# Quest chunk-select attention into a capacity-limited MoE: bounds a round later, first loads on two queues, key casts on ScalarE, expert rows turned one ahead

## Chip, core and metric

One Trainium2 chip, one core. The metric is device time in microseconds (us) of one execution of the kernel. "TensorE clock" below is the clock that the throttle granted, as a share of full speed, as the profile records it.

## The reference

Attention first, for B = 4, H = 8, S = 768, D = 64. Keys are cut into 24 chunks of 32. For each query, each chunk has an upper bound of its score, and only the six chunks with the highest bound (among those that the causal mask allows) are attended to. Then a mixture of experts, top-1 of 8, where each expert keeps the 80 tokens of highest gate weight and all other rows of the output are zero.

```python
ub = sum(maximum(q[..., None, :] * k_min, q[..., None, :] * k_max), -1)   # chunk bounds
ub = where(causal, ub, -1e9); top = argsort(ub)[..., -6:]
scores = q @ k.T / sqrt(64), kept where chunk in top and query >= key
x = softmax(scores) @ v                     # reshaped to 3072 x 512
logits = x @ w_gate; expert = argmax(logits); gate = softmax(logits)[expert]
for e in range(8):
    idx = the 80 tokens of expert e with the highest gate
    out[idx] = gate[idx] * (relu(x[idx] @ w1[e]) @ w2[e])   # F = 1024
```

## The kernel before

**Units of work.** The 32 heads are worked in 8 quads of four heads (g = 0 to 7), two quads to a batch entry. The 768 queries of a head are three thirds of 256 (t = 0, 1, 2), and each pair of a third and a pair of 128-key blocks is a round: one round for t = 0, two for t = 1, three for t = 2. So a quad has six rounds (r = 0 to 5) and the kernel 48 (rd = 6g + r). The third is complete at r = 0, 2 and 5.

**A round.** TensorE computes the scores of four heads (L352 to L373: keys by queries at L366, then at L370 a penalty of -30000 for chunks that were not selected, from `ind` and `PENT`) into four PSUM buffers, one for each head, of a pool `psS` that has just four. ScalarE takes the exponentials (L381, one for each head, into `E`); on the rounds of the diagonal, r = 0, 2 and 4, GpSimd masks them (L385). TensorE multiplies by the values of the round before (L390 to L403, into `ps_num`) and sums the denominators (L405 to L417, into `ps_den`). When a third is complete, ScalarE copies `ps_num` out (`npt`, L421); two rounds later the gate's logits are added from `npt` (`gate_rows`, L424, `DSB`), three rounds later VectorE gets denominators and logits (`scales`, L435 to L457, with the reductions `den` at L444), four rounds later TensorE turns the rows (`ps_xn`, L465), VectorE scales them (`x_nat`, L466) and they go to DRAM (L472). In odd quads, `scales` ends in `best` (L477: the row's maximum and the exponential `ex`, L489, on ScalarE) and, at the start of a later round, `gates` (L508) which writes `gmask`, `gs` and `slotrhs`.

**Preparing the next quad** (`prep`, L240) goes on beside this, with the keys and queries that the DMA has laid out as `kn` and `qn`:

- K step f (f = 0, 1): VectorE turns half of the keys (L250, 32x32 transposes, `kT`), GpSimd casts them to bf16 in another element order (`KB`, L266; its input has a stride of 32 elements), VectorE takes minimum and maximum over each chunk (L270). f = 0 is issued in r = 0, f = 1 in r = 1.
- Q step f: VectorE turns queries (L250, `qT`), ScalarE takes their positive part (`qp`, L276), GpSimd casts (`QB`, L278). Both in r = 2.
- `bound` (L294): 1152 small matmul instructions over the 8 quads (L310), into the same four `psS` buffers as the scores, and four transposes by VectorE (`ub`, L314). In r = 3, between `value` and `denom`.
- `rank` (L316): VectorE takes the eight highest bounds of each query and compares (`PEN`, L320). In r = 4.
- `unselect` (L324): TensorE turns `PEN` (`ps_pen`, L327), ScalarE copies it (`PENT`, L329). In r = 5, ahead of `value`.

`KB`, `QB`, `PEN` and `PENT` have two copies each, one for even and one for odd quads. `kT`, `qT`, `qp` have one.

**Loads.** All loads of keys, queries and values (L218 to L238) and the zero fill of the output (`zero_fill`, L130, 12 DMAs of 512 KB at r = 3, 4, 5 of quads 1 to 4) are issued by SyncE; weights of 1 MB a piece by GpSimd (L145, `load_whole` at r = 2 and 4, `late_weights` from rd 40 on, into tiles that are spent by then, the zero tile among them). The first keys and the first queries are loaded in three parts of four DMAs (L873, L874), and quad 0's keys are turned by thirds.

**Selecting while attention runs.** After quads 3 and 5, three generators sort the gate weights: `lanes1` (L571) sorts 96 lanes 128 wide, `lanes2` (L581) 64 lanes 160 wide, `lanes3` (L592) 40 lanes 288 wide. Each step is one VectorE maximum of eight and one replacement (L550, L552), and ten steps give 80 values. A generator is appended four rounds after the round that completed its third, and four steps are issued at each round's end (L951). From rd 42 (`FREEZE`) on, `freeze` (L611) has the threshold `ps_tau` and the places of the first three batch entries.

**The tail.** After the last round: `turn_new` (L706), `weigh1`, `rows`, `turn_new(2)`, `weigh2` (L785: TensorE spreads gates over rows, VectorE and GpSimd compare and count, `ps_idx` at L824 gives the indices of the rows kept). Then GpSimd gathers each expert's 80 rows (`X`, L976); `hidden` (L980) turns them on TensorE (`ps_XT`, L984), copies them on ScalarE (`XT`, L987) and multiplies by w1 (`ps_H`, L994); `result` (L1004) multiplies by w2 (`ps_Y`, L1008), scales (`Y`, L1011) and scatters (L1013). The order on TensorE is hidden(0), hidden(1), result(0), hidden(2), result(1) and so on.

**Who sets the order.** The order of TensorE and of SyncE's queue is the program's order throughout, VectorE's too until the last round (L870 to L872, L955). ScalarE's and GpSimd's instructions are put in order by the scheduler, each as its engine and its inputs are estimated to be ready. In the changed kernel as built, the scheduler puts both key casts of quad 1 ahead of round 0's exponentials; from quad 1 on it puts r = 0's cast ahead of that round's exponentials, right behind `PENT`, and r = 1's cast behind `npt`, ahead of r = 1's exponentials. In even quads both `qp` stand ahead of r = 3's exponentials; in odd quads the first stands ahead of r = 2's, and the second, with `npt`, behind r = 3's.

## Time and profile before

| what | value |
|---|---|
| two timed runs | 344.68 and 346.19 us, median 345.44 |
| the profiled execution | 341.36 us; span of the trace 339.6 us |
| mean granted clock of TensorE | 0.936 |
| half clock (0.5) | 67.18 to 70.59, 101.31 to 104.72, 224.19 to 227.60, 237.84 to 244.67, 275.39 to 278.80, 285.63 to 306.11 us |
| first score of rd 0 | 21.72 us |
| start of quads 1 to 7 (row turn at r = 0) | 50.1, 80.0, 112.25, 144.3, 174.2, 204.15, 245.0 us |
| first rows gathered, first `ps_H` | 296.69, 300.36 us |
| idle time of TensorE in gaps over 0.2 us | 53.3 us |
| longest of these gaps within the quads | 4.60 us at 234.48, 3.18 at 270.93, 2.77 at 98.80, 2.31 at 133.90, 1.99 at 264.33, 1.94 at 220.44 |
| in the tail | 3.02 us at 284.83, 3.33 at 291.71, 3.34 at 296.00, then 0.52 to 0.59 for each expert |
| `gmask` (VectorE, L522) | 0.18 us, but 3.70 at 92.06 and 4.06 at 155.84, while GpSimd ran the cast of `QB` |
| DMA | 47.82 MB, 141 GB/s over the span |

How to read the profile: PE is TensorE's matmuls, PEld its weight loads, DVE is VectorE, ACT ScalarE, POOL GpSimd, SP SyncE, and a trailing q means an engine's sequencer or queue. L366 is line 366 of the kernel. A row of the page's slices has 40 digits, the busy share of each fortieth of the span in tenths; PEclk is the granted clock in the same way. A row of waits reads: the waiting engine and its operation, who ended the wait, the total in us, how many, and the longest. A row of a timeline: start, length, engine, line, operation, out<-in, shape, how many, and in brackets the idle time of the engine before it with what ended it ("issue" is no wait that the trace shows).

### The profile page before, as it was taken

What the parts mean: (1) busy time and instruction counts of PE and PEld (TensorE: products, weight loads), DVE (VectorE), ACT (ScalarE), POOL (GpSimd) and SP (SyncE); (2) the same over time, 40 slices, a digit from 0 to 9 for tenths busy, and PEclk for the clock granted to TensorE, in tenths of its full rate; (3) what the DMA queues carried; (4) which work ended last, traced back from release to release, by engine and by line L of the source; (5) the groups of instructions that cost most, each with busy time, mean ns of one, the idle gap of its engine ahead of it and who ended that gap; (6) DMA issues with size and microseconds to landing.
All of it is one profiled execution on the core that took longest, in us unless ns stands there. A gap on an engine that the chain in (4) does not pass through costs nothing. (4 is left out here: it accounts for less than half of the span.)

```text
span 339.6 us, 12569 instructions
## 1 busy us (share of the span) xinstructions
PE 270.0 (80%) x5316; PEld 169.8 (50%) x5316; DVE 198.2 (58%) x697; ACT 141.8 (42%) x325; POOL 150.1 (44%) x315
## 2 busy tenths in 40 slices
PE   0349999799969986999999899766899675468881
PEld 0226666466636654565555566443456343255550
DVE  3666248358754754389796478976964845412230
ACT  1126356626723752566257347344164225412220
POOL 6936227635732562368118344664062101072222
PEclk9999999989998999999999999979599978559998
DMA  3799207995998299759949955699963001021121
GB/s 109 167 220 210 48 2 152 224 266 168 225 235 266 63 228 282 180 145 218 271 157 226 220 111 128 100 154 181 189 97 66 33 1 64 1 58 41 41 58 30
DMA packets 59367, 47.82 MB, mean 141 GB/s; under 512 B 27974, under 2 KB 51654, under 8 KB 59312
## 3 DMA queue, kind: packets, MB, share of 16 engines
q1 hardware_dynamic: 45776, 28.36, 33.3%
q0 software_dynamic: 13536, 18.67, 31.4%
q8 instruction: 41, 0.67, 0.9%
q14 instruction: 14, 0.11, 0.1%
HBM read 53.10 MB, written 10.76 MB: 188 GB/s over the span
## 5 line engine op out<-in xcount | busy, mean ns | idle before, releaser
L381 ACT ACTIVATE E<-ps_S 128x384 f32<-128x384 f32 (+1 forms) x192 | 91.5, 550 | 70.0 <-PE ps_S L370 70.0
L398 PE MATMUL ps_num<-E,vn 128*32 128x256 f32 (+1 forms) x1536 | 93.6, 365 | 0.8 <-issue 0.8
L398 PEld LDWEIGHTS ps_num<-E,vn 128*32 128x32 f32 x1536 | 51.2, 112 | 31.4 <-issue 5.6
L385 POOL TENSOR_SCALAR_AFFINE_SELECT E<-E 128x256 f32<-128x256 f32 x96 | 38.7, 434 | 52.0 <-ACT E L381 51.8
L414 PE MATMUL ps_den<-E,ones 128*32 128x256 f32 (+1 forms) x768 | 56.0, 371 | 4.0 <-issue 2.8
L414 PEld LDWEIGHTS ps_den<-E,ones 128*32 128x32 f32 x768 | 29.1, 116 | 19.9 <-issue 7.2
L266 POOL CAST KB<-kT 128x768 bf16<-128x768 f32 x16 | 25.1, 1570 | 30.3 <-DVE kT L250 21.0
L366 PE MATMUL ps_S<-QB,KB 32*128 32x256 bf16 (+1 forms) x768 | 35.3, 264 | 0.8 <-ACT E L381 0.8
L466 DVE TENSOR_TENSOR x_nat<-ps_xn,rec 128x512 bf16<-128x512 f32 x24 | 16.5, 687 | 27.3 <-PE ps_xn L465 22.4
L370 PE MATMUL ps_S<-PENT,ind 32*128 32x256 bf16 (+1 forms) x384 | 25.1, 257 | 2.7 <-issue 2.3
L278 POOL CAST QB<-qT 128x768 bf16<-128x768 f32 x16 | 24.4, 1545 | 3.6 <-DVE qT L250 3.5
L314 DVE STREAM_TRANSPOSE ub<-ps_u 128x160 f32<-128x160 f32 x32 | 8.3, 318 | 26.9 <-PE ps_u L310 26.9
L366 PEld LDWEIGHTS <-KB 32*128 32x128 bf16 x768 | 16.4, 94 | 14.9 <-issue 14.0
L276 ACT ACTIVATE qp<-qT 128x640 f32<-128x640 f32 x16 | 11.7, 749 | 19.8 <-DVE qT L250 19.5
L250 DVE STREAM_TRANSPOSE kT<-kn 128x768 f32<-128x768 f32 (+1 forms) x17 | 15.7, 923 | 6.8 <-DMA kn<-in_k_dram 6.7
L310 PE MATMUL ps_u<-ind,later 32*32 32x160 bf16 x128 | 6.4, 245 | 16.0 <-DVE later L79 8.0
L310 PE MATMUL ps_u<-qT,KMM 32*32 32x160 f32 x512 | 14.3, 444 | 6.0 <-DVE qT L250 6.0
L421 ACT ACTIVATE npt<-ps_num 128x512 f32<-128x512 f32 x24 | 14.8, 615 | 10.0 <-PE ps_num L398 10.0
L465 PE MATMUL ps_xn<-ident_f,npt 128*128 128x128 f32 x96 | 16.7, 300 | 0.9 <-DVE lg_h L451 0.7
L310 PE MATMUL ps_u<-qp,KMM 32*32 32x160 f32 x512 | 17.3, 446 | 0.0
L1013 POOL DMA_INDIRECT out_dram<-Y,sidx x8 | 7.4, 919 | 22.0 <-DVE Y L1011 13.3
L489 ACT ACTIVATE ex<-sh 128x16 f32<-128x16 f32 x12 | 2.6, 215 | 34.6 <-DVE sh L486 34.6
(217 smaller groups left out, 420.2 us busy)
## 6 DMA issues: line engine op xcount, KB each, us to landing
w<-in_moe_w_dram POOLq DMA_DIRECT2D x11, 1024.0 KB, 13.4
vn<-in_v_dram SPq DMA_DIRECT2D x32, 192.0 KB, 3.4
out_dram<-zero_tile SPq DMA_DIRECT2D x12, 512.0 KB, 12.0
kn<-in_k_dram SPq DMA_DIRECT2D x28, 192.0 KB, 6.9
qn<-in_q_dram SPq DMA_DIRECT2D x28, 192.0 KB, 9.0
x_dram<-x_nat SPq DMA_DIRECT2D x12, 257.0 KB, 3.0
kn<-in_k_dram SPq DMA_DIRECT2D x12, 64.0 KB, 1.9
qn<-in_q_dram SPq DMA_DIRECT2D x12, 64.0 KB, 1.9
```

Source lines behind the costliest of these rows:

```text
L250: nc.vector.transpose(out=dst[:, fs, 32 * xs.start:32 * xs.stop].rearrange("p f (x t) -> p x f t", t=CHUNK), in_=src[:].rearrange("p c (i ...
L266: nc.gpsimd.tensor_copy(out=straight(KB[s][:, f, :]), in_=natural(kT[:, f, :]))
L278: nc.gpsimd.tensor_copy(out=straight(QB[s][:, f, :]), in_=natural(qT[:, f, :]))
L310: nc.tensor.matmul(out=ps_u[h][32 * j:32 * (j + 1), :, :], lhsT=lhsT, rhs=rhs[rs, j], start=(w == 0), stop=(w == 2 and f == 1), skip_group ...
L366: nc.tensor.matmul(out=ps_S[h][:, m, 0:wid], lhsT=KB[s][rs, w, keys], rhs=QB[s][rs, w, q0:q0 + wid], start=(w == 0), stop=False, skip_grou ...
L370: nc.tensor.matmul(out=ps_S[h][:, m, lo - q0:wid], lhsT=ind[rs, keys], rhs=PENT[s][rs, lo - P:q0 + wid - P], start=False, stop=True, skip_ ...
L381: nc.scalar.activation(out=E[:].rearrange("p m q -> p (m q)")[:, 0:last], in_=ps_S[h][:].rearrange("p m q -> p (m q)")[:, 0:last], func=my ...
L385: nc.gpsimd.affine_select(out=E[:, :, 0:P], in_=E[:, :, 0:P], compare_op=ALU.is_ge, fill=0.0, base=0, pattern=[[0, 2], [1, P]], channel_mu ...
L398: nc.tensor.matmul(out=NUM[q0:q0 + 32, a, c0:THIRD], lhsT=nats[(g, "vn")][:, kb, 2 * a + r, 32 * f:32 * (f + 1)], rhs=Es[rd][2 * a + r][:, ...
L414: nc.tensor.matmul(out=dn[q0:q0 + 32, c0:THIRD], lhsT=ones32[:, a, :], rhs=Es[rd][2 * a + r][:, m, 0:wid], start=(i == 0 and x == 0), stop ...
L465: nc.tensor.transpose(ps_xn[:, j, a, :], npt[:, a, j * P:(j + 1) * P], ident_f32[:])
L466: nc.vector.tensor_tensor(out=xbuf[(b, t)][:, :, P * gi:P * (gi + 1)].bitcast(BF16).rearrange("p j (k d) -> p j k d", d=HEAD_D), in0=ps_xn ...
```

## The change

- The first loads are six DMAs of 128 KB for the keys on SyncE's queue and six for the queries on ScalarE's.
- The cast of `KB` is an activation (Copy) on ScalarE instead of a GpSimd copy.
- Q step 0 is issued in r = 2 and Q step 1 in r = 3; `bound` in r = 4, `rank` in r = 5, `unselect` at the end of r = 5, behind `denom`.
- `gates` is called at the end of the round before the one at whose start it stood. Generators are appended a round earlier, and their steps (3 or 4 a round) are issued between the `after` list and `value`.
- `lanes1` also sorts its own merge of 160 values (32 lanes), and `lanes2` sorts 128 wide (32 lanes) and merges.
- The two reductions of `den` become one.
- The zero fill is issued at the even rounds 16 to 38.
- 31 matmuls of 512 columns that compute nothing that is used (`idle`, into the spent `ps_num`): ten ahead of `turn_new(2)`, ten ahead of `ps_idx`, eleven behind it.
- The turn of an expert's rows is issued one expert ahead, behind `hidden(e)` and ahead of `result(e - 1)`.

```diff
@@ -217,16 +217,17 @@
 
-        def load(g, src, name, parts=1):
+        def load(g, src, name, engine=None):
             dst = qkp.tile([P, QBLK, 4 * HEAD_D], F32, name=name)
-            n = QBLK // parts
-            for i in range(parts):
+            if engine:
+                for c in range(QBLK):
+                    engine.dma_start(out=dst[:, c, :], in_=src[4 * g:4 * g + 4, :, c, :])
+            else:
                 for h in range(4):
-                    nc.sync.dma_start(out=dst[32 * h:32 * (h + 1), n * i:n * (i + 1), :],
-                                      in_=src[4 * g + h, :, n * i:n * (i + 1), :])
+                    nc.sync.dma_start(out=dst[32 * h:32 * (h + 1), :, :], in_=src[4 * g + h])
             nats[(g, name)] = dst
 
-        def load_k(g, parts=1):
-            load(g, k4, "kn", parts)
+        def load_k(g, engine=None):
+            load(g, k4, "kn", engine)
 
-        def load_q(g, parts=1):
-            load(g, q4, "qn", parts)
+        def load_q(g, engine=None):
+            load(g, q4, "qn", engine)
 
@@ -265,3 +266,4 @@
             def keys(f):
-                nc.gpsimd.tensor_copy(out=straight(KB[s][:, f, :]), in_=natural(kT[:, f, :]))
+                nc.scalar.activation(out=straight(KB[s][:, f, :]), in_=natural(kT[:, f, :]),
+                                     func=mybir.ActivationFunctionType.Copy)
                 kv = kT[:, f, :].rearrange("p (c i j t) -> p c j i t", i=4, j=4, t=8)
@@ -442,5 +444,4 @@
             dv = ps_dT[:].rearrange("p j (w r c) -> p j c r w", w=2, r=2)
-            for a in range(2):
-                nc.vector.tensor_reduce(out=den[:, :, a, :], in_=dv[:, :, a],
-                                        axis=mybir.AxisListType.X, op=ALU.add)
+            nc.vector.tensor_reduce(out=den[:], in_=dv[:, :, 0:2], axis=mybir.AxisListType.X,
+                                    op=ALU.add)
             rec = small.tile([P, 2, 4], F32, name="rec")
@@ -565,3 +566,3 @@
         L1 = cand[0][0:96, P:P + CAP]
-        S2, L2 = lane(0, 64, 208, 160), lane(0, 64, 368, CAP)
+        S2, L2 = lane(0, 32, 208, 160), lane(0, 32, 368, CAP)
         S3, L3 = lane(0, 40, 448, 288), lane(0, 40, 736, CAP)
@@ -575,6 +576,6 @@
             nc.vector.tensor_copy(out=back, in_=rev(cand[0][32:64, P:P + CAP]))
-            nc.vector.tensor_tensor(out=S2[0:32, 0:CAP], in0=L1[0:32, :], in1=back, op=ALU.max)
-            nc.vector.tensor_copy(out=S2[0:32, CAP:160], in_=L1[64:96, :])
-            nc.gpsimd.memset(cand[0][32:64, 208 + P:208 + 160], -1.0)
+            nc.vector.tensor_tensor(out=S2[:, 0:CAP], in0=L1[0:32, :], in1=back, op=ALU.max)
+            nc.vector.tensor_copy(out=S2[:, CAP:160], in_=L1[64:96, :])
             nc.gpsimd.memset(S3, -1.0)
+            yield from sort_lanes(S2, L2)
 
@@ -582,5 +583,5 @@
             copied(cand[0][32:64, 208:208 + P], turned(12, 4)[:])
-            yield from sort_lanes(S2, L2)
+            yield from sort_lanes(cand[0][32:64, 208:208 + P], cand[0][32:64, 368:368 + CAP])
             nc.vector.tensor_copy(out=back, in_=rev(cand[0][32:64, 368:368 + CAP]))
-            nc.vector.tensor_tensor(out=M3, in0=L2[0:32, :], in1=back, op=ALU.max)
+            nc.vector.tensor_tensor(out=M3, in0=L2, in1=back, op=ALU.max)
             for i in range(4):
@@ -784,2 +785,7 @@
 
+        def idle(n):
+            for _ in range(n):
+                nc.tensor.matmul(out=NUM[:].rearrange("p a q -> p (a q)"), lhsT=ident_bf[:],
+                                 rhs=ties[:, 0:2 * THIRD], start=True, stop=True)
+
         def weigh2():
@@ -823,2 +829,3 @@
                                     op=ALU.is_equal)
+            idle(10)
             ps_idx = misc([CAP, 2, NEXP], F32, "ps_idx")
@@ -831,2 +838,3 @@
                                  start=False, stop=(c == NEWB - 1), skip_group_check=True)
+            idle(11)
             left = selp.tile([CAP, NEXP], F32, name="left")
@@ -872,4 +880,4 @@
         with tc.manual_schedule(engines=by_hand | {mybir.EngineType.DVE}):
-            load_k(0, 3)
-            load_q(0, 3)
+            load_k(0, nc.sync)
+            load_q(0, nc.scalar)
             nc.sync.dma_start(out=wg_sb[:], in_=moe_w_gate.rearrange("(t r) e -> r t e", r=P))
@@ -890,4 +898,2 @@
                     eg, et = ends[rd - 4]
-                    if eg % 2 == 1:
-                        gates(eg // 2, et)
                     before.append(lambda e=ends[rd - 4]: rows(*e))
@@ -901,8 +907,6 @@
                         after.append(u["K"][1])
-                    elif r == 2:
-                        after += u["Q"]
-                    elif r == 4:
-                        after.append(u["rank"])
+                    elif r in (2, 3):
+                        after.append(u["Q"][r - 2])
                     elif r == 5:
-                        after.append(u["unselect"])
+                        after.append(u["rank"])
                 if r == 1 and 1 <= g < NQUAD - 1:
@@ -913,4 +917,4 @@
                     load_q(g + 2)
-                if r in (3, 4, 5) and 1 <= g <= 4:
-                    zero_fill(3 * (g - 1) + r - 3)
+                if 16 <= rd < 40 and rd % 2 == 0:
+                    zero_fill((rd - 16) // 2)
                 if r in (2, 4) and 1 <= g <= NPRE or r == 2 and g == NPRE + 1:
@@ -927,2 +931,6 @@
                     fn()
+                if merges:
+                    for _ in range((3, 4, 4, 3, 4, 4)[r]):
+                        if merges and next(merges[0], merges) is merges:
+                            merges.pop(0)
                 if rd == FREEZE:
@@ -937,3 +945,3 @@
                     value(rd - 1)
-                if r == 3 and g + 1 < NQUAD:
+                if r == 4 and g + 1 < NQUAD:
                     u["bound"]()
@@ -946,10 +954,11 @@
                         ends[rd - 1] = (gl, t)
-                if rd - 4 in ends:
-                    make = {(3, 2): lanes1, (5, 1): lanes2, (5, 2): lanes3}.get(ends[rd - 4])
+                if r == 5 and g + 1 < NQUAD:
+                    u["unselect"]()
+                if rd - 3 in ends:
+                    eg, et = ends[rd - 3]
+                    if eg % 2 == 1:
+                        gates(eg // 2, et)
+                    make = {(3, 2): lanes1, (5, 1): lanes2, (5, 2): lanes3}.get(ends[rd - 3])
                     if make:
                         merges.append(make())
-                if merges:
-                    for _ in range(4):
-                        if merges and next(merges[0], merges) is merges:
-                            merges.pop(0)
         with tc.manual_schedule(engines=by_hand):
@@ -962,2 +971,3 @@
             rows(*last)
+            idle(10)
             turn_new(2)
@@ -979,4 +989,5 @@
 
-        def hidden(e):
-            w1 = weights[(e, 0)]
+        XTs = {}
+
+        def turn_rows(e):
             ps_XT = psX.tile([P, 4, CAP], BF16, space=bass.MemoryType.PSUM, tag="x", name="ps_XT")
@@ -985,4 +996,8 @@
                                     ident_bf[0:CAP, 0:CAP])
-            XT = mp.tile([P, 4, CAP], BF16, name="XT")
-            nc.scalar.activation(out=XT[:], in_=ps_XT[:], func=mybir.ActivationFunctionType.Copy)
+            XTs[e] = mp.tile([P, 4, CAP], BF16, name="XT")
+            nc.scalar.activation(out=XTs[e][:], in_=ps_XT[:], func=mybir.ActivationFunctionType.Copy)
+
+        def hidden(e):
+            w1 = weights[(e, 0)]
+            XT = XTs.pop(e)
             HT = mp.tile([P, 8, CAP], BF16, name="HT")
@@ -1018,4 +1033,7 @@
         held = None
+        turn_rows(0)
         for e in range(NEXP):
             HT = hidden(e)
+            if e + 1 < NEXP:
+                turn_rows(e + 1)
             if held is not None:
```

## The prediction

> **What bounds the kernel now.** I read the page first, then the waits, the timeline of two quads, and the stretches of the tail.
>
> ```profile
> PE 270.0 (80%) x5316; PEld 169.8 (50%) x5316; DVE 198.2 (58%) x697; ACT 141.8 (42%) x325; POOL 150.1 (44%) x315
> ...
> PEclk9999999989998999999999999979599978559998
> ...
> issue 1%; POOLq 0%; DMA 0%
> ```
>
> TensorE is the fullest engine; the clock falls to half around slices 28 and 34-35. The chain of waits covers 1% of the span, so I followed TensorE's idle time instead. The waits name who ends it:
>
> ```profile
> POOL KB L266 <- DVE kT L250: 21.0, 7, 6.7
> ...
> PE ps_pen L327 <- DVE PEN L320: 8.1, 2, 4.6
> ...
> PE ps_u L310 <- ACT E L381: 7.7, 19, 1.9
> ...
> PE ps_H L994 <- ACT XT L987: 4.6, 8, 0.6
> ```
>
> The third row is what the move of the bounds is after, the fourth what turning rows ahead is after. The first is a wait that the change hands from GpSimd to ScalarE. Now the timeline of rounds 6 and 7:
>
> ```profile
> 49.50 0.66 PE L465 MATMUL ps_xn<-ident_f,npt 128*128 128x128 f32 x4
> ...
> 50.19 0.69 DVE L466 TENSOR_TENSOR x_nat<-ps_xn,rec 128x512 bf16<-128x512 f32 x1 [3.29 <-PE ps_xn L465]
> ...
> 50.80 1.64 ACT L381 ACTIVATE E<-ps_S 128x384 f32<-128x384 f32 x4 [1.15 <-PE ps_S L370]
> 50.80 0.97 DVE L250 STREAM_TRANSPOSE kT<-kn 128x768 f32<-128x768 f32 x1
> ...
> 51.90 1.59 POOL L266 CAST KB<-kT 128x768 bf16<-128x768 f32 x1 [6.42 <-DVE kT L250]
> ...
> 53.37 0.40 PE L366 MATMUL ps_S<-QB,KB 32*128 32x256 bf16 x8
> ...
> 53.53 0.97 DVE L250 STREAM_TRANSPOSE kT<-kn 128x768 f32<-128x768 f32 x1
> ```
>
> Round 6's exponentials run beside the turn of the keys; round 7's scores start at 53.37, 0.93 us after the exponentials' end at 52.44. These scores need the four PSUM buffers that the exponentials free, so 0.93 us is all the slack. Then, out of the timelines of TensorE and VectorE, the fetch gaps, a late key turn and an expert:
>
> ```profile
> 101.57 1.08 PE L414 MATMUL ps_den<-E,ones 128*32 128x128 f32 x11 [2.77 <-issue]
> ...
> 136.21 0.26 PE L370 MATMUL ps_S<-PENT,ind 32*128 32x256 bf16 x1 [2.31 <-issue]
> ...
> 211.29 0.96 DVE L250 STREAM_TRANSPOSE kT<-kn 128x768 f32<-128x768 f32 x1
> ...
> 308.41 1.31 PE L994 MATMUL ps_H<-XT,w 128*128 128x80 bf16 x32 [0.52 <-ACT XT L987]
> ```
>
> Two gaps of TensorE that nothing but its own issue ended, both in rounds with zero fill; a key turn that sorting pushed to 7.1 us after its round's row turn (3.4 in rounds 6 and 7); and 0.52 us that each expert waits for its turned rows. Last, a stretch of the tail: its length, busy time of TensorE, weight loads, VectorE, ScalarE and GpSimd, the granted clock, and the DMA's share and GB/s:
>
> ```profile
> 285.63:306.11 20.48, 9.75 (x100) 7.47 (x101) 7.04 (x34) 5.73 (x21) 8.94 (x16) 0.50 0.15 41
> ```
>
> 20.48 us at half clock, with TensorE busy for half of them.
>
> **The change, part by part.** The profiled execution took 341.36 us (span 339.6); the two runs' median is 345.44, so I add the sum to 345.44. Rounds are counted from 0, six to a quad; "r" is the round within its quad.
>
> *First loads.* Before, 24 DMAs of 64 KB leave SyncE 0.47 us apart, 0.80 to 12.02 us; from 2 to 12 us they move 141 GB/s, while 18 to 24 us moved 225. After, six of 128 KB leave each of two queues in about 3 us, so bandwidth binds: 1.57 MB at 225 to 269 GB/s is 5.8 to 7.0 us from 1.9 us, and the last third of the keys lands with the last queries, at 7.7 to 8.9 instead of 7.83. VectorE then has the third turn 0.71, four reductions 3.45, the indicator 0.55, and three query turns with `later` 2.2: 6.9 us, done at 14.6 to 15.5 where it was 14.32. +0.7 us. The Trainium skill ("DMA: Bandwidth & Descriptors", "Issuing engines are not separate DMA queues") says that queues share the same 16 DMA engines and that more of them only save issue time; it speaks against a gain here beyond the issue, and by it alone the term would be 0.
>
> *First casts.* The built ScalarE order puts both key casts of quad 1 ahead of round 0's exponentials. The second waits for a key turn that ends about 3.6 us after the first began (turn 0.97, two reductions 1.72, turn 0.97). Exponentials of round 0: 23.20 becomes about 26.3. GpSimd no longer holds round 0's masks back behind a 1.5 us cast (26.25 was value's start), so round 2 starts 0.65 us later than the first-load term makes it. +0.65.
>
> *Key casts on ScalarE, rounds r = 0 and 1.* No row shows this cast on ScalarE. The nearest is qp, 640 f32 wide: 749 ns, 0.70 apart, so 768 wide about 0.8; GpSimd's 1.57 us for the same strided shape is the upper bound. I take 0.8, the same engine. In r = 0 the cast waits for x_nat and the key turn: it runs 51.85 to 52.65, ahead of the exponentials, which start at 52.63 instead of 50.80. 1.83 less the slack 0.93 is about +1.0 us per quad, six quads. In r = 1 the second cast fits in the time so lost (+0). GpSimd saves 25.1 us, but no TensorE gap over 0.2 us was ended by GpSimd: 0.
>
> *Bounds a round later.* Odd quads lose the wait before ps_u (0.57 + 3 x 0.26 and 0.39 = 1.74 us in quad 1). New there: ex still holds round r = 3's exponentials, the second qp and npt now stand before r = 4's gate matmuls (+0.95), and VectorE ranks only in r = 5 after the gate chain, so the unselect at that round's end waits (+1.4). Net +0.15 for quads 1, 3, 5; with the cast +1.15 each. Even quads 2 and 4: both qp stand ahead of r = 3's exponentials and wait for the query turn moved to r = 3, which a gmask held by the query cast delays (3.70 us at 92.06, where 0.18 is usual); +1.25 at r = 4's scores, less 0.27 of old waits: +1.9 with the cast. Quad 0 +0.3. Quads 0 to 4 sum to 0.3 + 1.15 + 1.9 + 1.15 + 1.9 = 6.4; quad 4 gives back 0.7 of VectorE waits (166.07, 173.00): +5.7.
>
> *Sorting.* lanes1 grows by the sort of its own 160 wide merge: ten maxima and nine replacements of 0.77 us a pair, 7.3 us, while lanes2 shrinks from 160 to 128 wide (-1). The longer lanes1 runs into quad 5's r = 0 to 2. Four steps push the first key turn back by 1.85 us, three more the second by 2.3, four more the query turn by 3.1. Before, only GpSimd waited for such turns; now the casts stand before the exponentials, so TensorE does: 1.8 at round 31, 3.75 in all at round 32, 5.5 by round 33. Quad 5: 1.15 + 5.5 = +6.6. Quad 6 was already VectorE-bound (4.60 us before ps_pen, with a 3.8 us wait for a DMA in the third sort); a narrower second sort and no gmask stall bring its threshold 2.8 us earlier: -2.8.
>
> *Zero fill from round 16, one per two rounds.* Nothing waits for it but the weight load into its tile. The 2.77 and 2.31 us gaps coincide with instruction fetches (99.13, 133.92) in trains of three fills. Bounds: both gone (-5.1), or both stay (0). I take -5.1, as the trains are gone.
>
> *Rows turned one ahead.* The period of 3.77 us (308.41 to 312.18) loses its wait, hidden by the 1.9 us of the result matmuls, for experts 2 to 7: 6 x 0.58 = -3.5 us. Gather and scatter issues (0.92 us each) stay inside 3.2 us.
>
> *Idle matmuls.* If the clock stays full, then the work at half clock on the path shrinks by: spreads and what they delay 0.8, index 0.45, turn 0.15, hidden(0) 1.0, expert 1 1.1, first result 0.25: -3.75. Ten 512 wide matmuls last 2.2 us at full clock (8 in 1.90) and 4.3 at half (2 in 1.05, pipelined 0.43), against gaps of 3.02, 3.33, 3.34: if all run at half, +3.6. After filling there is still about 4.3 us idle in 13, as in the 70% busy stretch that ended in the drop at 285.63, so I take a partly held clock: -1.5. The Trainium skill ("TensorE: Matmul & The Clock Gate", "Part 1") has a free-running window of 3.4 us; the clock's records here change at such steps (3.41 us), and by the skill's rule that only a wholly idle window drops the clock, the term would be -3.75.
>
> Merging two den reductions saves 0.16 us of VectorE a quad-third, under cover: 0. Gates a round earlier: covered, 0.
>
> Sum: 0.7 + 0.65 + 5.7 + 6.6 - 2.8 - 5.1 - 3.5 - 1.5 = +0.75 us, so 346.2.
>
> **Rivals.** *The casts cost nothing*: if ScalarE reaches its exponentials in time after all, the six 1.0 and the 5.5 fall away: 346.2 - 11.5 = 334.7. For it: ScalarE is busy 42% and GpSimd's 25.1 us vanish; against it: the order above. *The cast is as slow as on GpSimd (slower)*: 0.75 more in r = 0 and in r = 1, where no slack is left, 6 x 1.5: 355.2. It decides from about 1.3 us per cast, seen on ScalarE's row of KB; for it, the stride of 32 elements in its input; against, qp's rate. *The idle matmuls run at half clock*: +3.0 in place of -1.5, 350.7. *The fetch gaps stay*, since keys, queries, values and weights alone saturate the DMA (share 1.16): 351.3.
>
> **How the numbers follow.** The mixed sum, with the last two rivals in it, 0.55, own range 341 to 352; casts free 0.28; slow cast 0.17. 2% is 6.9 us, about what a measurement of this kernel tells from no change: faster below 338.5, slower above 352.3. Faster takes the free casts (0.25 of 0.28) and 0.05 of the mixed case; slower the slow cast (0.15 of 0.17) and 0.05; the rest, 0.50, is the same. The range reaches to both outer cases: 334 to 355.5.
>
> **What would show it.** Round r = 1's scores starting 4.3 us after the row turn instead of 3.2; a KB row on ScalarE of 0.8 us; quad 5's r = 0 to 2 some 6 us longer; no issue gap over 2 us; expert period 3.2 us; granted clock in the tail between 0.5 and 1. I am wrong if ScalarE's exponentials do not wait for the casts, or if the tail gives more than 5 us.

## The result, and the profile after

The changed kernel takes 372.87 us (two runs, 372.44 and 373.3) against 345.44: a ratio of 1.079, 95% interval 1.068 to 1.091, so 23 to 31 us more. The prediction was 346.2 us, in a range of 334 to 355.5. The profiled execution took 372.44 us, span 370.6. Some runs of a kernel take over 1.5% longer than its fastest, and the ratios here and below leave them out, so that a ratio can differ a little from that of two medians. Where the 31.0 us between the two spans lie:

| stage (starts as in the table of before) | before, us | after, us | difference | the prediction's terms |
|---|---|---|---|---|
| to the first scores | 21.7 | 34.1 | +12.4 | +0.7 |
| first scores to quad 1 | 28.4 | 30.7 | +2.3 | +0.65 and +0.3 |
| quads 1 to 3 | 94.2 | 98.7 | +4.5 | +4.2, less 5.1 for gaps |
| quad 4 | 29.9 | 36.5 | +6.6 | +1.2 |
| quad 5 | 30.0 | 38.9 | +8.9 | +6.6 |
| quad 6 | 40.8 | 37.2 | -3.6 | -2.8 |
| quad 7 to the last scores | 24.6 | 27.3 | +2.7 | none |
| last scores to the end | 70.0 | 67.3 | -2.7 | -5.0 |

Three lines of the page of after: busy times, the granted clock, and the group of the key casts (mean ns of one behind the comma).

```profile
PE 282.0 (76%) x5345; PEld 167.2 (45%) x5347; DVE 200.9 (54%) x701; ACT 163.3 (44%) x341; POOL 124.1 (33%) x298
...
PEclk9998699999999999999978899899999986989995
...
L267 ACT ACTIVATE KB<-kT 128x768 bf16<-128x768 f32 x16 | 25.1, 1572 | 22.8 <-DVE kT L251 22.8
```

GpSimd has lost 26 us and ScalarE has got 21.5, and one cast takes 1572 ns on ScalarE, as long as the 1570 on GpSimd. TensorE's busy share fell from 80 to 76%: it waits more. The waits of after (us in all, how many, longest) say for what:

```profile
ACT KB L267 <- DVE kT L251: 22.8, 10, 9.1
...
DVE kT L251 <- DMA kn<-in_k_dram: 17.1, 3, 7.4
...
PE ps_den L416 <- ACT DSB L434: 9.4, 9, 3.3
...
PE ps_S L368 <- ACT E L383: 7.7, 16, 3.4
...
PE ps_pen L329 <- DVE PEN L322: 4.7, 3, 3.6
```

The wait for key turns has indeed gone from GpSimd to ScalarE. Of the old rows `ps_u <- E` (7.7 us) is gone and `ps_H <- XT` has shrunk from 4.6 to 1.3; TensorE waits 9.4 us for ScalarE's `DSB` (1.1 before) and, ahead of the scores, 7.7 for its `E` (0.8). The second row is the start: VectorE waits 17.1 us for the first keys. VectorE's timeline there, and the stretches of after (length, busy times of TensorE, weight loads, VectorE, ScalarE, GpSimd, then granted clock, DMA share of 16 engines, GB/s):

```profile
8.58 0.71 DVE L251 STREAM_TRANSPOSE kT<-kn 128x512 f32<-128x512 f32 x1 [7.38 <-DMA kn<-in_k_dram]
14.12 0.71 DVE L251 STREAM_TRANSPOSE kT<-kn 128x512 f32<-128x512 f32 x1 [4.83 <-DMA kn<-in_k_dram]
19.75 0.71 DVE L251 STREAM_TRANSPOSE kT<-kn 128x512 f32<-128x512 f32 x1 [4.92 <-DMA kn<-in_k_dram]
```

```profile
5.00:8.00 3.00, 0.00 (x0) 0.00 (x0) 0.00 (x0) 0.00 (x0) 0.39 (x1) 1.00 0.27 96
8.00:12.00 4.00, 0.00 (x0) 0.00 (x0) 0.71 (x1) 1.28 (x1) 0.00 (x0) 1.00 0.27 96
```

The third key turn starts at 19.75 us where it started at 7.95. Both queues together move 96 GB/s with a DMA share of 0.27: 0.27 x 16 = 4.3 engines busy. One queue of 64 KB pieces moved 141 GB/s before, with a share of 0.51. At 96 GB/s the 1.57 MB of both loads take 16.4 us, and the six DMAs leave SyncE in 8.2 us and ScalarE in 9.3.

The timeline of quad 1, r = 0 and 1, in the changed kernel:

```profile
66.46 1.59 ACT L267 ACTIVATE KB<-kT 128x768 bf16<-128x768 f32 x1 [1.35 <-DVE kT L251]
...
67.95 1.62 ACT L383 ACTIVATE E<-ps_S 128x384 f32<-128x384 f32 x4
...
68.48 1.52 PE L368 MATMUL ps_S<-QB,KB 32*128 32x256 bf16 x8 [0.18 <-ACT E L383]
...
69.91 1.63 ACT L267 ACTIVATE KB<-kT 128x768 bf16<-128x768 f32 x1
...
71.39 1.13 ACT L383 ACTIVATE E<-ps_S 128x512 f32<-128x512 f32 x2
...
72.84 0.86 PE L416 MATMUL ps_den<-E,ones 128*32 128x256 f32 x16 [0.56 <-ACT DSB L434]
```

Each cast ends just as the exponentials begin. The eight score matmuls at 68.48 stretch to 1.52 us (0.40 before), since each head's buffer comes free late. From first score to first score, r = 0 takes 3.73 us (3.28 before) and r = 1 5.52 (3.64): 2.3 us for a pair of casts, most of it in r = 1. Quad 4's +6.6 is 2.2 of the same kind and 4.2 in r = 3 and 4, where the bounds' matmuls stand still for 3.31 us (191.72, shown further below) and the clock is at half from 190.4 to 197.3.

### The profile page after: what moved, and what is told of

It reads as the page before. It is cut to its first block, busy times and chain, and to the rows that moved or that the text cites. A ratio compares the mean times of both kernels' runs of the same rounds, so it can differ in the third digit from the quotient of the medians.

```text
span 370.6 us, 12603 instructions
## 1 busy us (share of the span) xinstructions
PE 282.0 (76%) x5345; PEld 167.2 (45%) x5347; DVE 200.9 (54%) x701; ACT 163.3 (44%) x341; POOL 124.1 (33%) x298
## 5 line engine op out<-in xcount | busy, mean ns | idle before, releaser
L416 PE MATMUL ps_den<-E,ones 128*32 128x256 f32 (+1 forms) x768 | 53.7, 373 | 12.6 <-ACT DSB L434 9.4
L368 PE MATMUL ps_S<-QB,KB 32*128 32x256 bf16 (+1 forms) x768 | 45.2, 270 | 10.0 <-ACT E L383 7.7
L416 PEld LDWEIGHTS ps_den<-E,ones 128*32 128x32 f32 x768 | 25.6, 114 | 30.6 <-ACT DSB L434 13.5
L267 ACT ACTIVATE KB<-kT 128x768 bf16<-128x768 f32 x16 | 25.1, 1572 | 22.8 <-DVE kT L251 22.8
L368 PEld LDWEIGHTS <-KB 32*128 32x128 bf16 x768 | 21.2, 95 | 27.4 <-issue 26.1
L280 POOL CAST QB<-qT 128x768 bf16<-128x768 f32 x16 | 24.6, 1543 | 14.5 <-DVE qT L251 13.6
L467 DVE TENSOR_TENSOR x_nat<-ps_xn,rec 128x512 bf16<-128x512 f32 x24 | 16.4, 685 | 23.6 <-PE ps_xn L466 23.6
L372 PE MATMUL ps_S<-PENT,ind 32*128 32x256 bf16 (+1 forms) x384 | 27.4, 264 | 1.9 <-issue 1.5
L251 DVE STREAM_TRANSPOSE kT<-kn 128x768 f32<-128x768 f32 (+1 forms) x17 | 15.7, 922 | 17.1 <-DMA kn<-in_k_dram 17.1
L445 DVE TENSOR_REDUCE den<-ps_dT 128x8 f32<-128x16 f32 x24 | 4.0, 168 | 34.0 <-PE ps_dT L442 34.0
L312 PE MATMUL ps_u<-ind,later 32*32 32x160 bf16 x128 | 2.4, 247 | 25.7 <-DVE later L79 25.7
L278 ACT ACTIVATE qp<-qT 128x640 f32<-128x640 f32 x16 | 11.9, 748 | 21.2 <-DVE qT L251 21.2
L539 POOL TENSOR_SCALAR slotrhs<-oh,pcol 128x16 bf16<-128x16 bf16 x9 | 3.0, 331 | 45.4 <-DVE oh L505 45.4
L551 DVE MAX8 cand<-cand 96x8 f32<-96x128 f32 (+3 forms) x40 | 13.3, 334 | 8.7 <-ACT cand L564 7.7
```

What stands on the lines that cost most here:

```text
L251: nc.vector.transpose(out=dst[:, fs, 32 * xs.start:32 * xs.stop].rearrange("p f (x t) -> p x f t", t=CHUNK), in_=src[:].rearrange("p c (i ...
L267: nc.scalar.activation(out=straight(KB[s][:, f, :]), in_=natural(kT[:, f, :]), func=mybir.ActivationFunctionType.Copy)
L280: nc.gpsimd.tensor_copy(out=straight(QB[s][:, f, :]), in_=natural(qT[:, f, :]))
L312: nc.tensor.matmul(out=ps_u[h][32 * j:32 * (j + 1), :, :], lhsT=lhsT, rhs=rhs[rs, j], start=(w == 0), stop=(w == 2 and f == 1), skip_group ...
L368: nc.tensor.matmul(out=ps_S[h][:, m, 0:wid], lhsT=KB[s][rs, w, keys], rhs=QB[s][rs, w, q0:q0 + wid], start=(w == 0), stop=False, skip_grou ...
L372: nc.tensor.matmul(out=ps_S[h][:, m, lo - q0:wid], lhsT=ind[rs, keys], rhs=PENT[s][rs, lo - P:q0 + wid - P], start=False, stop=True, skip_ ...
```

## The experiments

Each ratio is to the kernel before, timed on the same chip, with its 95% interval; us are medians. Round lengths run from the first score of a round to that of the next. The last control shows what such an interval leaves out: the kernel before, timed against itself, gave 1.011 (1.003 to 1.019), so differences under about 1% are not read from times alone here.

**The first loads.** Four kernels tell the shape of the loads from the number of queues.

```diff
+ # a1: 24 DMAs of 64 KB (one head, 32 partitions), all on nc.sync
+ # a2: the same 24, keys on nc.sync, queries on nc.scalar
+ # a3: the new 12 of 128 KB (four heads, 128 partitions), all on nc.sync
+ # e1: the kernel before, with only the new loads on two queues
```

> The changed kernel with the first loads as they were: 24 DMAs of 64 KB, all on SyncE's queue. Theory (the shape of the new loads costs the start): keys and queries moved at 96 GB/s in the changed kernel with a DMA share of 0.27, against 136 to 145 GB/s before, and the first scores came 12.4 us later (34.1 instead of 21.7). So here the first scores start at 21.5 to 23 us and the whole takes 372.9 - 12 = about 360.5 us. Rival (the late start is made up later by other waits): above 368 us.

> The changed kernel with the 64 KB pieces of before (32 partitions, one head each), but keys on SyncE's and queries on ScalarE's queue. Theory (the shape: four heads as the outermost index of the source keep about four of sixteen DMA engines busy): first scores at 22 us or earlier, DMA share from 2 to 8 us above 0.5, about 358 to 361 us. Rival (two queues at a time slow each other): first scores still at about 34 us, DMA share about 0.27, about 372 us.

> The changed kernel with the new 128 KB loads of four heads, but all on SyncE's queue. Theory (shape): still 85 to 100 GB/s and a DMA share of about 0.27 to 18 us; first scores at 31 to 35 us, about 370 to 374 us. Rival (two queues slow each other): 140 GB/s and more, first scores at about 22 us, about 360 us.

> The kernel before with one part of the change: the first loads, six of 128 KB on each of two queues. Theory (96 GB/s from the start, whatever else is in the kernel): first scores at 33 to 35 us instead of 21.7, later quads unchanged, 11 to 14 us over before, 3.2 to 4%. Rival (the loads collide with the rest of the change only): first scores before 26 us, under 5 us over before.

Measured: a1 357.34 us, 1.029 (1.022 to 1.036), first scores at 21.8; a2 360.05, 1.042 (1.038 to 1.047), first scores at 23.6; a3 363.80, 1.049 (1.043 to 1.055), first scores at 29.3; e1 358.13 against 344.63, 1.038 (1.028 to 1.047), first scores at 35.2. The stretches of a3 and of a2:

```profile
8.00:12.00 4.00, 0.00 (x0) 0.00 (x0) 0.72 (x2) 0.00 (x0) 0.00 (x0) 1.00 0.27 96
```

```profile
2.00:8.00 6.00, 0.00 (x0) 0.00 (x0) 1.26 (x2) 0.10 (x1) 3.23 (x11) 1.00 0.79 215
```

One queue with the new shape moves the same 96 GB/s at the same share, and two queues with the old shape move 215: it is the shape, and the number of queues does not matter to it. Nor is it the size of the packets, 1 KB in both shapes: in the changed kernel 4 to 6 of them are under way at any time from 5 to 12 us, in a1 up to 16 from 3 to 10 us. The first scores come earlier in a3 than in the changed kernel (29.3 instead of 34.1, and not the 31 to 35 expected) since the keys no longer share the four engines with the queries: the third key turn starts at 11.99 us. The Trainium skill ("DMA: Bandwidth & Descriptors", "Why a DMA increments its semaphore by 16 and not by 1") says that a DMA of these queues runs on the largest number of engines, 16 at most, that divides the outermost size of both its sides; the new source has four heads outermost, and the share of 0.27 (4.3 engines) agrees. a2 also shows that faster first loads gain nothing here: the third key turn starts at 10.13 us (7.92 in a1), because keys and queries now arrive together and the keys are wanted first.

**The key casts.** Undone in the changed kernel, alone in the kernel before, and made quick.

```diff
- nc.scalar.activation(out=straight(KB[s][:, f, :]), in_=natural(kT[:, f, :]), func=Copy)
+ # a4: nc.gpsimd.tensor_copy(out=straight(KB[s][:, f, :]), in_=natural(kT[:, f, :]))
+ # b2, with a1's loads: nc.scalar.activation(out=KB[s][:, f, :], in_=kT[:, f, :], func=Copy)
+ # d1: the kernel before, with only the casts on nc.scalar
```

> The changed kernel with the casts of the keys back on GpSimd. Theory (the casts, 1.57 us each on ScalarE, stand ahead of the exponentials in r = 0 and 1): quad 1 lost 0.45 + 1.9 us there, seven quads with the sorting's push on quads 5 and 6 some 16 to 20 us: 353 to 358 us. Rival (the bounds moved a round and the sorting make the loss of quads 1 to 6, the casts are hidden): 369 to 373 us.

> The kernel before with one part of the change: key casts on ScalarE. Theory (1.57 us each, ahead of the exponentials in r = 0 and 1 of seven quads; undoing it in the changed kernel gave 8 to 12 us): 7 to 12 us over before, 2 to 3.5%. Rival (it costs only beside the longer sort and the moved bounds): under 4 us.

> The changed kernel with old loads (357.3 us), casts of the keys on ScalarE, but reading and writing in order instead of with a stride of 32 elements (the keys' order is then wrong, so the output is not the reference's). Theory (the stride makes the cast slow): 0.8 us per cast, the price of each quad's r = 0 and 1 falls by 1.5 us, 345 to 350 us. Rival (the engine or the width makes it slow): 1.57 us per cast and 357 us.

Measured: a4 360.80 us, 1.042 (1.038 to 1.046), 13 us under the changed kernel's 1.079; d1 357.42 against 343.73, 1.042 (1.028 to 1.057), so the casts alone cost 9 to 20 us, at or above the 7 to 12 expected; its span is 354.7 us, the control's 344.8. b2 357.39 against 350.09, 1.016 (1.002 to 1.029), where a1 with the slow casts was 1.029. The groups of the casts in b2:

```profile
L269 ACT ACTIVATE KB<-kT 128x768 bf16<-128x768 f32 x16 | 13.4, 844 | 23.2 <-DVE kT L253 23.2
```

Read in order the cast takes 844 ns, with the stride 1572. So the stride nearly doubles it on ScalarE; no run has the cast in order on GpSimd. In quad 1, r = 0 takes 3.48 us and r = 1 4.28; with the slow cast (a1) 3.73 and 5.51, and without a cast on ScalarE (b1) 3.48 and 3.64. So a cast of 0.84 us costs nothing in r = 0 and 0.64 us in r = 1. The time falls by about 1.3%, 4.6 us, less than the 7 to 12 expected; the two intervals overlap, and the two kernels ran on different chips.

**Both undone.** The rest of the change, without the two.

```diff
+ # b1: the changed kernel with a1's loads and a4's casts
```

> The changed kernel with both of its costly parts undone: first loads as before, key casts on GpSimd. Theory (the two parts explain the loss, and the rest of the change is worth about nothing): 357.3 - 12.6 = about 345 us, within 1% of before. Rival (the bounds a round later and the longer first sort cost as much as the tail gains give back or more): 350 us or more, with quads 1 to 6 each longer than before.

Measured: 353.18 against 351.12 us, 1.005 (1.001 to 1.010); one of the ten executions took 834.85 us, and why is not known. The rest of the change together is worth about nothing. Its quads 5 and 6 are 41.3 and 36.1 us (30.0 and 40.8 before).

**The tail.** From b1, and alone.

```diff
+ # b3: b1, with turn_rows(e) right ahead of hidden(e)
+ # b4: b1, without the idle matmuls
+ # b5: b1, scatter of odd experts to a scratch tensor
-                out=out[:], out_offset=IndirectOffsetOnAxis(ap=sidx[:, e:e + 1], axis=0),
+                out=(aside if e % 2 else out)[:], out_offset=...
+ # d3: the kernel before, with turn_rows ahead and the idle matmuls
```

> As the kernel with old loads and GpSimd casts, but an expert's rows are turned right before its own hidden layer, as before. Theory (the eight scatters of the output wait for one another, 3.38 us apart, 25.4 us from first to last in the changed kernel and 25.8 before, so the tail's end is set by the first scatter): TensorE's last result comes 3.5 us later, the end at most 1 us later. Rival (the prediction's: TensorE's period sets the end): the end is 3.5 us later.

> As the kernel with old loads and GpSimd casts, but without the 31 idle matmuls. Theory (they hold the clock up, and what they shorten lies ahead of the first scatter): from the first hidden layer to the first scatter 8.4 us (6.4 with them), and 0.5 to 1 us more ahead of the indices: the end 2 to 3 us later. Rival (the idle matmuls only fill gaps that nothing on the path needed): within 1 us.

> As the kernel with old loads and GpSimd casts, but the scatters of odd experts go to a scratch tensor, so that the output lacks these experts' rows; no scatter waits for the one just before it. Theory (the scatters' mutual wait sets the end): scatters 3.0 us apart like TensorE's experts, first to last about 21.2 us instead of 25.4, the end about 4 us earlier. Rival (the scatters are paced by something else, GpSimd or the results): still 25 us from first to last, no change of the end.

> The kernel before with two parts of the change: expert rows turned one ahead, and the idle matmuls. Theory (the chain of eight scatters sets the end; only what makes the first scatter earlier counts): TensorE's last result 5 to 7 us earlier after the first hidden layer where the clock holds, first scatter up to 2 us earlier, the whole 0 to 2.5 us under before. Rival (the prediction's two terms): 5 us under before, 1.4%.

Measured: b3 353.46 us, 1.007 (1.002 to 1.012): TensorE's last result comes 3.6 us later after the first hidden layer (37.6 against 34.0), the end does not. b4 352.44, 1.008 (1.004 to 1.011): no difference to b1 that can be told, so the 2 to 3 us of its theory are not confirmed. b5 348.58, 0.994 (0.988 to 1.000): 4.0 us (1.14% of 351.12) under b1. d3 342.08 against 343.73, 1.000 (0.996 to 1.004): the last result comes 6.6 us earlier after the first hidden layer than before (25.05 against 31.65), the time is the same within the interval. GpSimd's timelines say why. First the changed kernel's scatters, then b5's:

```profile
343.63 0.94 POOL L1028 DMA_INDIRECT out_dram<-Y,sidx  x1 [2.51 <-DVE HT L1012]
348.87 0.91 POOL L1028 DMA_INDIRECT out_dram<-Y,sidx  x1 [4.30 <-DMA out_dram<-Y,sidx]
352.24 0.91 POOL L1028 DMA_INDIRECT out_dram<-Y,sidx  x1 [2.47 <-DVE Y L1026]
355.63 0.91 POOL L1028 DMA_INDIRECT out_dram<-Y,sidx  x1 [2.47 <-DVE HT L1012]
```

```profile
323.22 0.93 POOL L1030 DMA_INDIRECT aside<-Y,sidx  x1 [2.06 <-DVE Y L1028]
326.23 0.91 POOL L1030 DMA_INDIRECT out_dram<-Y,sidx  x1 [2.08 <-DVE Y L1028]
329.25 0.91 POOL L1030 DMA_INDIRECT aside<-Y,sidx  x1 [2.11 <-DVE Y L1028]
```

Scatters to one tensor follow 3.38 us apart, each waiting for the one before it to land, whatever ended last by name: eight of them take 25.4 us from first to last issue in the changed kernel, 25.8 before, 25.2 in b1. In b5 they follow TensorE's experts, 3.02 us apart, and take 19.7 (21.2 expected). TensorE's period fell from 3.77 to 3.02 us, below the scatters' 3.38, so the chain of scatters sets the end: what counts is its first scatter, and whether one of them lands late. Such a late landing stands behind the step from 343.63 to 348.87 above (the scatter's last packet ends 3.95 us after its issue began, that of the others 2.1 to 2.3); 17 of the 20 profiles have one, but b3, b4 and b5 have none, and its cause is open. So the equal ends of b1, b3 and b4 are partly chance: in b3 the scatters follow TensorE, 3.70 to 3.92 us apart (25.9 in all), and in b4's profile (a run of 358.48 us) the first comes 1.3 us later after the last scores than in b1 (46.0 against 44.7), but the eight take only 23.7. Before, the chain already ran 1.9 us behind the last result (last `Y` written at 332.80, last scatter issued at 334.65).

What the idle matmuls did is seen in the stretch between the last round's rows and the first hidden layer; the kernel before, then the changed one:

```profile
284.17:300.36 16.19, 5.25 (x36) 3.09 (x36) 7.52 (x38) 6.05 (x24) 4.72 (x12) 0.55 0.09 27
```

```profile
318.78:333.74 14.96, 11.23 (x64) 5.27 (x66) 7.52 (x38) 6.10 (x24) 4.67 (x12) 0.89 0.10 30
```

The granted clock goes from 0.55 to 0.89 and the stretch is 1.2 us shorter. From the first hidden layer to the first scatter it is 6.4 us instead of 8.4, where the turned rows help too.

**Bounds, sorting, zero fill.** Each undone from b1, and put alone or together into the kernel before.

```diff
+ # c1: b1, query step 1, bound, rank, unselect in their old rounds
+ # c2: b1, the three sorts, their steps and the gates as before
+ # c3: b1, zero_fill at r = 3, 4, 5 of quads 1 to 4
+ # d2: the kernel before, with the three sorts, their steps and the gates as changed
+ # e2: d2, with query step 1, bound, rank, unselect as changed
```

> As the kernel with old loads and GpSimd casts (0.5% above before), and query step 1, bounds, ranks and unselect back in their old rounds. Theory (the move of the bounds is worth about nothing: it saves the old wait, 1.7 us in an odd quad, and pays it back as later exponentials and a later unselect): within 2 us of that kernel, 0 to 1% above before. Rival (the move is what makes quads 1 to 5 longer): 3 us or more below it, at or under before.

> As the kernel with old loads and GpSimd casts, and the three sorts, their steps' places and the gates as before. In that kernel quad 5 took 41.3 us (29.9 before) and quad 6 36.1 (40.8): 6.7 us more in the two. Theory (the longer first sort on VectorE, ahead of key turns and ranks, does it): quads 5 and 6 take 70 to 73 us together instead of 77.4, and the whole comes 4 to 7 us lower, 0.7 to 1.5% under before. Rival (the bounds a round later do it): 76 us or more for the two, no change of the whole.

> As the kernel with old loads and GpSimd casts, and the zero fill in the old rounds, three in a row. TensorE's gaps over 1 us that only its own issue ends summed to 5.1 us before, to 8.0 in that kernel and to 9.6 in the changed one. Theory (the gaps come with any load on the DMA and only move): the same within 1%, gaps of 4 to 10 us in all. Rival (the prediction's: the trains of fills make them): 5 us longer than that kernel, with gaps over 2 us in quads 2 and 3.

> The kernel before with one part of the change: the three sorts, the places of their steps and of the gates. Theory (the longer first sort pushes the key and query turns of quad 5 back, the shorter second one and earlier gates help quad 6): quad 5 about 36 to 40 us instead of 30, quad 6 about 36 instead of 41: 1 to 5 us over before. Rival (VectorE's work is the same in all and hidden): within 1 us of before.

> The kernel before with two parts of the change: the bounds a round later (with query step 1, ranks and unselect) and the three sorts with their places. Theory (the two belong together: with the sort's steps early, the key and query turns come late, and the later bounds give them the time): 0 to 4 us over before, 0 to 1.2%, where the sorting alone was 2.8% over. Rival (each has its price and they add): 10 us or more over, 3% or more.

Measured: c1 364.39 against 350.09 us, 1.046 (1.035 to 1.058), far above both its forecasts; c2 356.60, 1.022 (1.012 to 1.033), above b1 where 4 to 7 us below it were expected, although quads 5 and 6 fell to 33.1 and 42.2 us (75.3 together); c3 354.26, 1.016 (1.003 to 1.028), with a span of 351.0 us where b1 has 350.8; d2 353.81 against 343.73, 1.028 (1.017 to 1.038), 6 to 13 us where 1 to 5 were expected, quads 5 and 6 35.8 and 39.7 us in its profile, a run of 357.16 us; e2 350.83 against 344.63, 1.020 (1.013 to 1.026), 4.6 to 9.1 us, between its theory (0 to 4) and its rival (10 or more), quads 5 and 6 39.5 and 35.6.

Two things follow. First, the early, longer sort lengthens quad 5 wherever it stands, by 6 to 11 us against the kernel before, while quad 6 is up to 5 us shorter. The two together take 70.8 us before, and 75.5 (d2), 75.2 (e2), 77.3 (c1) and 77.4 (b1) with the new sort: the place of the bounds makes no difference to them. In quad 5 of the changed kernel, VectorE's last lines ahead of the turn, and ScalarE's and TensorE's lines:

```profile
206.37 0.30 DVE L553 MATCH_REPLACE8 cand<-cand 32x160 f32<-32x160 f32 x1
206.59 0.96 DVE L251 STREAM_TRANSPOSE kT<-kn 128x768 f32<-128x768 f32 x1
```

```profile
207.59 1.55 ACT L267 ACTIVATE KB<-kT 128x768 bf16<-128x768 f32 x1 [1.32 <-DVE kT L251]
```

```profile
210.44 1.10 PE L416 MATMUL ps_den<-E,ones 128*32 128x256 f32 x16 [1.95 <-ACT DSB L434]
```

Sort steps hold the key turn to 206.59, the cast and with it the exponentials and `DSB` wait behind it, and TensorE waits 1.95 us for `DSB`. In b1, with the casts on GpSimd, the same wait is 5.15 us, because there the query's `qp` stands on ScalarE ahead of the exponentials and of `DSB`, and it cannot start until VectorE has turned the queries:

```profile
188.23 0.74 ACT L279 ACTIVATE qp<-qT 128x640 f32<-128x640 f32 x1 [6.59 <-DVE qT L253]
...
190.05 1.93 PE L417 MATMUL ps_den<-E,ones 128*32 128x256 f32 x16 [5.15 <-ACT DSB L435]
```

So the turn's lateness reaches TensorE by the one or the other. Second, sorting and bounds do not add: the bounds without the new sort (c2) and the sort without the new bounds (d2, c1) were each 2 to 5% over before, both together 0.5% (b1) to 2% (e2). Since e2's and d2's intervals touch and equal kernels differ by 1%, it is not settled whether the two parts fit together or each is merely slow. The profiles show where the pairs that differ in the bounds alone part: from the start of quad 7 to the last scores c1 takes 31.1 us at a mean clock of 0.84 and b1 25.1 at 1.00, d2 29.5 at 0.88 and e2 25.7 at 1.00 (before: 24.6 at 1.00). Half clock costs TensorE 5.0 us there in c1 (0.16 x 31.1) and 3.5 in d2 (0.12 x 29.5), an estimate that comes near the differences of 6.0 and 3.8; what lowers the clock is open, and with it why c1 is 4.6% over.

The zero fill: gaps over 1 us that only TensorE's own issue ended sum to 5.1 us in the profile of before, 9.6 in the changed kernel, 8.0 in b1 and 7.1 in c3, which has the old fill. Over all profiles they sum to 3.6 to 6.2 where the bounds are in their old rounds (before, c1, d0 to d3, e1) and to 5.5 to 9.8 where they are moved. The longest of the changed kernel's stands inside the bounds' own matmuls:

```profile
191.72 0.81 PE L312 MATMUL ps_u<-qp,KMM 32*32 32x160 f32 x22 [3.31 <-issue]
```

So the fill's place does not make the gaps. c1 shows it best: with the new fill and the old bounds, its two gaps stand at the same two instructions as those of before (101.57 and 136.21 there):

```profile
100.84 0.80 PE L417 MATMUL ps_den<-E,ones 128*32 128x128 f32 x11 [2.29 <-issue]
...
135.90 0.26 PE L373 MATMUL ps_S<-PENT,ind 32*128 32x256 bf16 x1 [2.07 <-issue]
```

The moved bounds lengthen them in both pairs that differ in nothing else, from 4.4 us (c1) to 8.0 (b1) and from 4.3 (d2) to 9.4 (e2), with one profile each. In all 20 profiles together there are 72 such gaps, and each of them ends 1.1 to 1.6 us after an instruction fetch has landed (a packet on the DMA's queue 8, one about every 7 us); a moment picked at random lies in such a band 9% of the time. So these times say that TensorE waits there for instructions; what makes just these fetches late no run shows.

**The control.** The kernel before, run as if it were another.

```diff
+ # d0: no edit
```

> The kernel before, unchanged, for a profile on this chip and as a measure of the scatter between equal kernels. Theory (TensorE's 7 us stall behind the first hidden layer, in the six profiles of the last two chips, belongs to the chip): if the other kernels of this call show it, this one does too. Rival (it belongs to the changed tail): only the kernel with the changed tail shows it. The ratio should be 1.00 within 0.5%.

Measured: 345.77 against 343.73 us, 1.011 (1.003 to 1.019). None of the kernels timed beside it (d1, d2, d3) had the stall either, so its question stayed open.

No kernel that computes the reference came out faster than before.

## Why the prediction was wrong

**First loads (+0.7; measured +12.4, alone +12.9 (9.6 to 16.2)).** This step failed, and it is the largest single stage of the loss. It took "six of 128 KB leave each of two queues in about 3 us, so bandwidth binds", with 225 to 269 GB/s. The 225 is from a stretch whose loads had another shape, and 269 stands in no row. The rate was 96 GB/s, because four heads are outermost in the source and about four of the engines work. The rule of the Trainium skill ("DMA: Bandwidth & Descriptors", "Issuing engines are not separate DMA queues") that queues share the engines, which the prediction weighed, held (a3 against the changed kernel: the same rate); the rule on the number of engines, named above with the first experiments, was not weighed and would have told.

**Key casts (0.8 us taken, 1.57 measured; +1.0 a quad taken, +2.3 in quad 1).** The order on ScalarE was right, casts ahead of exponentials, and so was that TensorE then waits. Two steps failed. Wrong was the row: `qp` reads in order, and of the two bounds it was the farther one in what matters, the stride. In order the cast would have taken 844 ns (b2). Wrong was also where the price falls: 1.0 us in r = 0 and, as "the second cast fits in the time so lost (+0)", nothing in r = 1. Measured are 0.45 and 1.88 us in quad 1 of the changed kernel. With the cast at 0.84 us (b2) r = 0 is 0.20 us longer than before (as in b1, without the cast) and r = 1 0.64, so at the price assumed for a cast the 1.0 a quad would have come out nearly right, but by luck. The slack of 0.93 us was counted to the end of all four exponentials, but the scores start as soon as the first head's buffer is free. In the sum the 1.0 stands for five quads, not for the six that the text names; quad 6 has only the -2.8. The rival "slow cast" was the true case, from 1.3 us on as it said: it put 355.2 on the whole, and with 11.7 more for the first loads (12.4 less 0.7) comes to 366.9, 6 us short of the measurement.

**Sorting (+5.5 and -2.8).** Measured +8.9 and -3.6 for quads 5 and 6, with casts at twice the price taken. Right in sign, and in that late turns on VectorE do it; wrong in that they reach TensorE by the casts alone: with the casts on GpSimd quad 5 is as long, by `qp` (b1). **Bounds**: not to be told apart from sorting by these runs; the two together, 4.6 us by the prediction's terms without casts (0.3 + 3 x 0.15 + 2 x 0.9 - 0.7 + 5.5 - 2.8), measured 6.9 (4.6 to 9.1, e2). Of the two VectorE waits that quad 4 was to give back, the one at 166.07 was none: only TensorE's own issue ended it.

**Fetch gaps (-5.1; measured +4.5).** The step "as the trains are gone" failed: the trains of fills do not make the gaps. With the trains gone but the bounds in place both gaps stay (c1), and the old fill in c3 leaves the sum as it is. The instruction fetches that the prediction saw beside them are what TensorE waits for.

**Rows ahead (-3.5; measured about 0 at the end).** TensorE's period fell as forecast (3.2 forecast, 3.02 measured). That "Gather and scatter issues (0.92 us each) stay inside 3.2 us" failed as a reason: the scatter's issue takes 0.92 us, but the next waits for it to land, 3.38 us in all. The trace of before showed it, in the scatters from 321.31 on (324.70, 328.08, 331.45).

**Idle matmuls (-1.5).** Not confirmed. In the profile of the changed kernel the first scatter comes 2.3 us earlier after the last scores (36.9 against 39.2) and the end 2.7, but that has the turned rows in it, and the times do not show it: d3, with both, reaches from -1.2 to +1.4 us, and b4's difference to b1 is no difference. A partly held clock was the right choice (0.89). The rule that the prediction cites, that only a wholly idle window drops the clock, does not fit these traces: in the kernel before it fell at 285.63 us after 3.41 us in which TensorE was busy for 2.31, in the changed kernel at 330.4 after 3.4 with 1.72 busy.

The parts measured alone, each by its ratio, sum to 12.9 (e1) + 14.5 (d1) + 6.9 (e2) + 0.1 (d3) = 34.4 us, against 27.4 (23 to 31) for the whole. Their intervals, taken together, leave about 7 us either way, so the parts account for the loss, and whether they overlap cannot be told. The two large terms are the loads and the casts.

## What to carry to other kernels

Before merging DMAs into larger ones, look at the outermost index of both sides and, in the trace, at the DMA share beside the GB/s: a low share with a full queue is shape, not issue. Price a moved operation from a row with the same access pattern, not the same engine, and ask what now stands behind it in that engine's order. Before shortening an engine's period, look which chain ends the stage: here the scatters, 3.38 us apart, would have swallowed any gain beyond 0.4 us an expert (3.77 less 3.38).

## What the runs showed of the hardware

A cast of 128 x 768 that reads with a stride of 32 elements takes 1570 ns on GpSimd (before) and 1572 on ScalarE (changed), and 844 on ScalarE in order (b2).

In the eight profiles from two of the chips (b1, b3, b4, b5 and c1, c2, c3, b2) TensorE stood still 5.3 to 7.2 us behind the first hidden layer. In b1 it waited for ScalarE, whose copy `HT` started at 312.96 after 7.81 us of idle time that the trace puts down to nothing in the kernel, 0.7 us after the last packet of the eight gathers (312.30):

```profile
313.77 2.29 PE L1010 MATMUL ps_H<-XT,w 128*128 128x80 bf16 x32 [7.12 <-ACT XT L999]
```

On those two chips the kernel before took 351.12 and 350.09 us, on the others 343.73 to 346.54. The twelve other profiles do not have the stall, and no profile of the kernel before from those two chips exists, so its cause is open.
